# Output weights converted during the expert stage, weight sums kept for a second pass, rounds alternating at two entries, activation sums moved to VectorE

## The chip, the cores and the metric

The kernel runs on one core of one Trainium2 chip. The metric is the device time of one execution in microseconds (us), the median of several runs. The engines are TensorE (PE, matrix products), VectorE (DVE), ScalarE (ACT), GpSimd (POOL) and SyncE (SP, which here issues nearly all DMAs, in order). SBUF is the on-chip memory, PSUM the banks in which PE accumulates and from which the other engines read.

## The reference

Three stages follow one another, all in float32, on 1792 tokens of width 768:

```
scores = q @ k.T / sqrt(64) - log(448);  attn = sigmoid(scores) @ v          # 4 x 12 heads
e = argmax(x @ w_gate);  y = gate * (relu(x @ w1[e]) @ w2[e])                # 8 experts, width 1024
g = y @ w_gate2;  out = (g * sigmoid(g) * (y @ w_val)) @ w_out               # width 1536
```

w_gate2, w_val and w_out reach the kernel as 64-bit numbers and are converted to float32 on the chip with integer operations. All large products are made as three products of a value split into a high and a low part ("hi" and "lo").

## The kernel before, in words

Every engine runs its instructions in the order in which the program issues them; that order is written out by hand. Five stretches follow one another in the trace: attention (0 to about 222 us), the expert stage (to 558 us), the gated layer in two passes over the tokens (558 to 918 us), and the output product (918 us to the end).

**Expert stage.** Tokens are gathered into slots of 128. `seq` lists weight chunks, first the 6 chunks of w1 (1024 wide) of a slot, then the 8 of w2 (768 wide) of the slot before. For each chunk `split_w` makes the high part on ACT (`whi`, L936) and the low part on DVE (`wlo`, L938), and `product` (L960) multiplies. Other work is hung on places of `seq` by `when`. Among it are five half slots of 64 tokens, whose matmuls (`bps`, L1066) need no splitting: they take PE's time and nothing of DVE or ACT.

**Gated layer.** It uses Strassen's method with 7 products for 8. A round r is one column pair of w_gate2 (even r) or w_val (odd r) against one half of the tokens; there are NR = 24 rounds, the first 12 (a pass) on tokens 0 to 895, the other 12 on the rest. Each of the 7 products n of a round is 9 matmuls of 448 columns (L805, banks pa, pb, pc, pd). `steps` lists the 168 products in the order in which PE makes them. Around each product stand: `load_item` (a weight tile `w` from DRAM, on SP), `sum_w` (POOL adds weight blocks to `sr`, L695), `prep` (ACT `wgh`, DVE `wgl`, L78 and L79, five products ahead), `split_x` (the high part `x` on ACT, the low part on DVE or POOL, L779, needed at each pass's first use of a product's activations), and `evac` and `finish_tile` behind a product (PSUM banks copied out or added, then the sigmoid `m`, then `m` times value, then `h`, which SP stores in `hd`). The activations come into `rx` by PE transposes (L753) and ACT copies; their Strassen differences are made by `sum_x` (L769), on POOL for the first pass and on DVE, 1344 wide, for the second.

**w_out.** The conversion of w_out has 12 pieces of 128x768. `load_o` loads one, `convert_o` runs three steps (one ACT operation L161, four DVE operations L162 to L172, one POOL multiplication L173), and SP stores the result in `wod`. The pieces are hung on products of the gated layer, from round 5 on, 9 products apart.

**PSUM banks.** pc and pd are held by two rounds at a time; the next pair's product into a bank waits until the last reader of the pair before has read it. For products 3 and 4 that reader is the DVE addition L859 into an SBUF tile `c`.

Of the kernel before, what the change touches and what calls it, by code (L numbers as in the profile page):

```python
# [22 lines left out]
def sigmoid_attention_moe_swiglu_kernel(  # L23
# [48 lines left out]
    wgd = dram.tile([2 * K2, P, DM], F32, name="wgd")  # L72

# [82 lines left out]
    def convert(r, u, w, eng=nc.gpsimd):  # L156
# [12 lines left out]
        def s2():  # L169
            nc.vector.scalar_tensor_tensor(u, lo, 29, u, op0=ALU.logical_shift_right,  # L170
                                           op1=ALU.bitwise_or)
            eng.tensor_scalar(w, w, TINY, None, op0=ALU.is_ge)  # L172
            nc.gpsimd.tensor_tensor(w, w, u.bitcast(F32), op=ALU.mult)  # L173

        return [s0, s1, s2]

    with ExitStack() as actx:
# [28 lines left out]
        fwt = const.tile([P, G, W], F32, name="fwt")  # L206
# [473 lines left out]
    witems = [(r, x) for r in range(NR) for x in range(2)]  # L680
    full = [max(place[r, n] for n in ORD) for r in range(NR)]

    def load_item(r, x):
        t = early.tile([P, DM], F32, tag="w", name="w", bufs=4)
        f = 2 * (r // 2 % NP) + x
        nc.sync.dma_start(t, wgd[(r % 2) * K2 + f])
        wraws[r, x] = t

    def a_block(r, i, k):
        return wraws[r, i - 1][:, (k - 1) * HK:k * HK]  # L690

    def sum_w(r, n):
        def made(m, x, y, op):
            t = early.tile([P, HK], F32, tag="sr", name="sr", bufs=4)
            nc.gpsimd.tensor_tensor(t, x, y, op=op)  # L695
            sums[r, m] = t

        if n == 6:
            made(1, a_block(r, 2, 1), a_block(r, 2, 2), ALU.add)
            made(2, sums[r, 1], a_block(r, 1, 1), ALU.subtract)  # L700
        elif n == 7:
            made(3, a_block(r, 1, 1), a_block(r, 2, 1), ALU.subtract)
        elif n == 3:
# [14 lines left out]
    def load_to(m):  # L718
        while state["load"] < min(m, len(witems)):
            load_item(*witems[state["load"]])  # L720
            state["load"] += 1

    def prep_to(m):
        m = min(m, len(steps))
        while state["sum"] < min(m + 4, len(steps)):
            sum_w(*steps[state["sum"]])
            state["sum"] += 1
        while state["prep"] < m:
            prep(*steps[state["prep"]])
            state["prep"] += 1  # L730

# [16 lines left out]
    def x_piece(p, t, j):  # L748
# [8 lines left out]
        nc.scalar.copy(rx[p][:, j // K3, t, j % K3], pt[:, :TH])  # L757

    def x_block(p, k, t):
        return rx[p][:, k - 1, t - 1]  # L760

    def sum_x(p, m, eng, t=None):
        x, y = {1: lambda: (x_block(p, 1, 2), x_block(p, 1, 1)),
                2: lambda: (x_block(p, 2, 2), tr[p, 1]),
                3: lambda: (x_block(p, 2, 2), x_block(p, 1, 2)),
                4: lambda: (x_block(p, 2, 1), tr[p, 2])}[m]()
        if t is None:
            t = {3: y, 4: x}[m]
        eng.tensor_tensor(t, x, y, op=ALU.subtract)  # L769
        tr[p, m] = t  # L770
# [66 lines left out]
    def evac(r, n):  # L837
# [177 lines left out]
    pre = [lambda: load_to(4)] + [lambda m=m: prep_to(m) for m in range(1, AHEAD + 2)]  # L1015
# [89 lines left out]

    def extra():
# [38 lines left out]
    def early_sums():  # L1145
        for m in (1, 2):
            sum_x(0, m, nc.gpsimd, yt([P, K3, TH], f"t{m}"))
        sum_x(0, 3, nc.gpsimd)

    when(1, L - 1, 7, early_sums)  # L1150
    when(1, L, 4, lambda: sum_x(0, 4, nc.gpsimd))
    with tc.manual_schedule():
# [94 lines left out]
        ot = {}  # L1247

        def load_o(f):
            ot[f] = yt([P, 2 * DM], "ro64", I32)  # L1250
            load_r64(ot[f], ("o", f))

        def convert_o(f, g):
            if g == 0:
                t = yt([P, 2, DM], "uw", I32)
                w = t[:, 1].bitcast(F32)
                ot[f] = (convert(ot[f], t[:, 0], w, nc.vector), w)
            parts, w = ot[f]
            parts[g]()
            if g == 2:  # L1260
                nc.sync.dma_start(wod[f], w)
                del ot[f]

# [5 lines left out]
        R1 = 2 * NP  # L1269
        def split_all(p, n, eng=nc.gpsimd):  # L1270
# [9 lines left out]
        def sum_next(m):  # L1280
            tag = {1: "hh", 2: "hh", 4: "hl"}.get(m)
            sum_x(1, m, nc.vector, None if tag is None else post.tile(
                [P, K3, TH], F32, tag=tag, name=f"t{m}", bufs=2))

        for m in range(1, 5):
            at_step(5 + m, 5, lambda m=m: sum_next(m))
# [27 lines left out]
        def advance(r, n):  # L1314
# [6 lines left out]
            load_to(4 + 2 * sum(m <= i + AHEAD for m in full))  # L1321
# [78 lines left out]
```

## Time and profile before

| | |
|---|---|
| median of 3 runs | 1107.53 us (1107.26 to 1107.55) |
| profiled execution | 1106.29 us, its span 1104.6 us |
| mean granted clock of PE over the span | 0.98 of full speed |
| PE busy | 1044.2 us, 95% of the span |
| DVE, ACT, POOL busy | 743.0, 566.5, 444.5 us |
| DMA | 199.22 MB, mean 180 GB/s |

How to read it: an engine's busy time is summed over the whole span, and the stretches differ. PE at 95% can still have short stretches in which it waits or runs at a lower clock; those are found by cutting the span into windows. In a window's row the first figure is its length, then come each engine's busy time and instruction count, then the clock granted to PE as a share of full speed, the busy share of the DMA engines, and what they moved.

### The profile page before, as it was taken

How to read it: one execution, taken by the hardware profiler on the slowest of the kernel's cores; microseconds unless marked ns; L12 is line 12 of the kernel's file. 1: busy time of each engine (PE TensorE's matmuls, PEld its weight loads, DVE VectorE, ACT ScalarE, POOL GpSimd, SP SyncE). 2: the span in 40 equal slices, each digit the busy share in tenths (PEclk: the TensorE clock that was granted, in tenths of full speed). 3: DMA queues.
4: the chain of work that ended last, by engine and by line, in shares of the span. 5: the costliest groups of instructions: out<-in, count | busy, mean ns of one | idle time of the engine just before them, and what ended most of it. 6: DMA issues, size and time to landing. Idle time of an engine off the chain costs nothing. (4 is left out here: it accounts for less than half of the span.)

```text
span 1104.6 us, 16743 instructions
## 1 busy us (share of the span) xinstructions
PE 1044.2 (95%) x5766; PEld 846.6 (77%) x5766; DVE 743.0 (67%) x1067; ACT 566.5 (51%) x860; POOL 444.5 (40%) x348
## 2 busy tenths in 40 slices
PE   8999999999999999999779998968999999999996
PEld 5555555477868777778669997867887888999996
DVE  4777777786767767766777679999899985111110
ACT  6676766376777776767554453463344453112110
POOL 3656566420131112010475446676657663111111
PEclk9999999999999999999889999988999999999998
DMA  7897986956687757596313435423535476322210
GB/s 211 260 292 237 277 250 197 353 163 197 229 306 269 256 175 236 205 365 187 125 59 128 141 105 176 134 86 120 176 134 176 134 205 196 97 86 86 89 68 29
DMA packets 144620, 199.22 MB, mean 180 GB/s; under 512 B 54208, under 2 KB 107456, under 8 KB 144528
## 3 DMA queue, kind: packets, MB, share of 16 engines
q1 hardware_dynamic: 137552, 168.93, 48.3%
q0 software_dynamic: 6048, 28.92, 7.0%
q8 instruction: 47, 0.77, 0.3%
q14 instruction: 45, 0.37, 0.1%
q10 hardware_dynamic: 928, 0.23, 0.1%
HBM read 207.27 MB, written 42.68 MB: 226 GB/s over the span
## 5 line engine op out<-in xcount | busy, mean ns | idle before, releaser
L938 DVE TENSOR_TENSOR wlo<-wraw,whi 128x768 fp32r<-128x768 f32 (+1 forms) x186 | 199.3, 1094 | 91.9 <-ACT whi L936 89.0
L936 ACT CAST whi<-wraw 128x768 fp32r<-128x768 f32 (+1 forms) x186 | 169.9, 927 | 97.8 <-PE yps L960 50.2
L1343 PE MATMUL po<-x,hh 128*128 128x384 f32 x588 | 131.5, 336 | 1.3 <-DVE h L833 0.7
L236 ACT ACTIVATE a<-sc,logs 112x896 f32<-112x896 f32 x96 | 92.0, 1019 | 60.1 <-PE sc L234 60.1
L79 DVE TENSOR_TENSOR hl<-ht,hh 128x1536 fp32r<-128x1536 f32 x14 | 24.6, 1758 | 124.8 <-ACT hh L78 124.8
L1343 PEld LDWEIGHTS po<-x,hh 128*128 128x128 f32 x588 | 104.8, 188 | 2.0 <-DVE h L833 1.1
L805 PE MATMUL pa<-x,wgh 128*128 128x448 f32 x288 | 87.8, 386 | 18.9 <-DVE m L829 10.9
L805 PE MATMUL pd<-x,wgh 128*128 128x448 f32 x288 | 87.7, 387 | 18.0 <-DVE c L852 17.5
L79 DVE TENSOR_TENSOR wgl<-sr,wgh 128x384 fp32r<-128x384 f32 x96 | 80.3, 842 | 13.1 <-ACT wgh L78 13.1
L805 PE MATMUL pc<-x,wgh 128*128 128x448 f32 x288 | 84.4, 373 | 3.8 <-POOL x L779 2.2
L78 ACT CAST hh<-ht 128x1536 fp32r<-128x1536 f32 x14 | 20.7, 1478 | 121.1 <-PE po L1343 121.1
L172 POOL TENSOR_SCALAR w<-w 128x768 f32<-128x768 f32 x24 | 55.3, 2303 | 60.4 <-ACT w L161 60.2
L1343 PE MATMUL po<-x,hl 128*128 128x384 f32 x294 | 77.8, 336 | 0.0
L805 PEld LDWEIGHTS pa<-x,wgh 128*128 128x128 f32 x288 | 55.6, 197 | 28.6 <-DVE m L829 14.2
L245 PE MATMUL pu<-a,vraw 112*64 112x448 f32 x384 | 77.5, 545 | 0.0
L1365 POOL DMA_INDIRECT out_dram<-ob,perm_c x13 | 20.9, 1606 | 139.9 <-ACT ob L1364 139.9
L805 PEld LDWEIGHTS pd<-x,wgh 128*128 128x128 f32 x288 | 55.6, 198 | 26.9 <-DVE c L852 17.7
L79 DVE TENSOR_TENSOR wgl<-w,wgh 128x384 fp32r<-128x384 f32 x72 | 65.2, 906 | 14.0 <-ACT wgh L78 14.0
L695 POOL TENSOR_TENSOR sr<-w 128x384 f32<-128x384 f32 x48 | 60.4, 1258 | 26.2 <-DMA w<-wgd 17.7
L78 ACT CAST wgh<-sr 128x384 fp32r<-128x384 f32 x96 | 48.8, 512 | 38.9 <-PE pd L805 25.0
L805 PEld LDWEIGHTS pc<-x,wgh 128*128 128x128 f32 x288 | 54.4, 190 | 9.8 <-POOL x L779 2.6
L853 POOL TENSOR_TENSOR c<-u,c 128x448 f32<-128x448 f32 x24 | 38.9, 1621 | 55.0 <-DVE c L852 55.0
(283 smaller groups left out, 2453.6 us busy)
## 6 DMA issues: line engine op xcount, KB each, us to landing
wraw<-in_moe_w_dram SPq DMA_DIRECT2D x108, 384.0 KB
wraw<-in_moe_w_dram SPq DMA_DIRECT2D x78, 512.0 KB
w<-wgd SPq DMA_DIRECT2D x48, 384.0 KB
ring<-in_moe_w_dram SPq DMA_DIRECT2D x30, 512.0 KB
ring<-in_moe_w_dram SPq DMA_DIRECT2D x40, 384.0 KB
hd<-h SPq DMA_DIRECT2D x48, 224.0 KB
ht<-hd SPq DMA_DIRECT2D x14, 768.0 KB
r<-in_moe_w_gate_dram SPq DMA_DIRECT2D x12, 768.0 KB
```

The lines of the kernel that those rows point to most:

```text
L78: nc.scalar.copy(hi, src)
L79: nc.vector.tensor_sub(lo, src, hi.bitcast(F32))
L172: eng.tensor_scalar(w, w, TINY, None, op0=ALU.is_ge)
L236: nc.scalar.activation(am[i][:, c], sc[:CP, :, :S], AF.Sigmoid, bias=logs[:CP], scale=SCALE)
L245: nc.tensor.matmul(pu[h * D:(h + 1) * D, :S], vt[:, h, c], a[:, c, h], start=(c == 0), stop=(c == C - 1))
L695: nc.gpsimd.tensor_tensor(t, x, y, op=op)
L805: nc.tensor.matmul(ps, st[:, a], mv[:, j], start=(j == 0 and m == 0 and n not in (2, 3, 4)), stop=(j == K3 - 1 and m == 2), skip_group_che ...
L853: nc.gpsimd.tensor_tensor(t, sb[r, "u"], t, op=ALU.add)
L936: nc.scalar.copy(hi[:, :w], r)
L938: nc.vector.tensor_sub(lo[:, :w0], r[:, :w0], hi[:, :w0].bitcast(F32))
L1343: nc.tensor.matmul(po[:, m, :HW], st[:, f], wo[f, m][mv], start=(f == 0 and x == 0), stop=(f == K2 - 1 and x == 2))
L1365: nc.gpsimd.indirect_dma_start(out=out[:, :], out_offset=bass.IndirectOffsetOnAxis(ap=perm_c[:, t:t + 1], axis=0), in_=ob[:, :], in_offset ...
```

## The change

Six things are edited.

- **w_out's conversion.** Nine of the 12 pieces (FO = 9) go to the expert stage, at 18 places of `seq` that have a half slot's matmuls (`spots`): two DVE operations at each, and the ACT operation at every second one. They work in a tile `room`, which uses the space that `rx` takes later. SP gets their loads (768 KB each) and stores (384 KB each) there. The other three stay in the gated layer, in the second pass, 14 products apart. The last step is one DVE operation instead of one of DVE and one of POOL.
- **Weight sums.** In the first pass SP stores each of the 48 sums in `wsd` (192 KB each), and in the second pass it loads them from there. POOL makes no sums in the second pass, and the second `w` tile of a round is loaded by half. `sr` has 6 buffers instead of 4, and `load_more` loads a tile as soon as the one four earlier has no reads left.
- **Order of products.** At the entry of both passes, and in the last pair of the first pass, the two rounds of a pair alternate (r, r+1, r, r+1, ...). The splits of the first pass's x are hung on rounds 0, and all are on DVE.
- **Activation sums.** They are made in pieces of 448 on DVE (`t_piece`) in both passes; the first is taken by DVE from the transposes in PSUM.
- **PSUM.** For n = 3 and 4 the addition goes back into the bank, and the sigmoid and both multiplications read the bank.
- `fwt`, a table of the attention, lies in another pool.

```diff
+    wsd = dram.tile([K2, 4, P, DM // 2], F32, name="wsd")
...
+        def s3():
+            nc.vector.scalar_tensor_tensor(w, w, TINY, u.bitcast(F32), op0=ALU.is_ge,
+                                           op1=ALU.mult)
...
+    ORD2 = (1, 6, 5, 7, 2, 4, 3)
+    R1 = 2 * NP
+    BOTH = (0, R1 - 2, R1)
     steps = [(r, n) for n in ORD[:1] + ORD[4:5] for r in range(2)]
-    steps += [(r, n) for r in range(2) for n in ORD if n not in (ORD[0], ORD[4])]
-    steps += [(r, n) for r in range(2, NR) for n in ORD]
+    steps += [(r, n) for n in ORD2 if n not in (ORD[0], ORD[4]) for r in range(2)]
+    for r in range(2, NR, 2):
+        if r in BOTH:
+            steps += [(r + x, n) for n in ORD2 for x in range(2)]
+        else:
+            steps += [(r + x, n) for x in range(2) for n in ORD]
...
-        def made(m, x, y, op):
-            t = early.tile([P, HK], F32, tag="sr", name="sr", bufs=4)
-            nc.gpsimd.tensor_tensor(t, x, y, op=op)
+        def made(m, f):
+            t = early.tile([P, HK], F32, tag="sr", name="sr", bufs=6)
+            at_ = wsd[r % R1, m - 1]
+            if r < R1:
+                x, y, op = f()
+                nc.gpsimd.tensor_tensor(t, x, y, op=op)
+            else:
+                nc.sync.dma_start(t, at_)
...
+        if m is not None and r < R1:
+            nc.sync.dma_start(wsd[r, m - 1], s)
...
+        if t == 1 and k == 0:
+            nc.vector.tensor_sub(x[:, 0, 1, jj], pt[:, :TH], x[:, 0, 0, jj])
+            tr[p, 1] = x[:, 0, 1]
+        else:
+            nc.scalar.copy(x[:, k, t, jj], pt[:, :TH])
...
+    def t_piece(p, m, jj):
...
+        nc.vector.tensor_sub(tr[p, m][:, jj], x[:, jj], y[:, jj])
...
-            t = et("c", 3)
-            V.tensor_add(t, bank(r, {3: "c", 4: "d"}[n]), sb[r, "u"])
+            t = bank(r, {3: "c", 4: "d"}[n])
+            V.tensor_add(t, t, sb[r, "u"])
...
+    FO = 9
...
+    spots = [BG0 + k * BGN + d for k in range(NH0) for d in (5, 11, 18, 25, 31)]
...
+    for f in range(FO):
+        for g in range(4):
+            when(*seq[spots[2 * f + g // 2]], lambda f=f, g=g: convert_o(f, g, get_o))
...
-    when(1, L - 1, 7, early_sums)
-    when(1, L, 4, lambda: sum_x(0, 4, nc.gpsimd))
...
-        for n, at_ in ((5, (1, 2)), (7, (0, 6)), (3, (0, 5)), (4, (0, 7))):
-            at_step(*at_, lambda n=n: split_all(0, n))
+        for n in ORD2[2:]:
+            if n != 2:
+                at_step(0, {5: 6, 7: 5, 4: 7, 3: 4}[n], lambda n=n: split_all(0, n))
...
-        for f in range(K2):
-            d = 9 * f
-            at_step(5, 4, lambda f=f: load_o(f), d)
-            for g in range(3):
-                at_step(6, 4, lambda f=f, g=g: convert_o(f, g), d + g)
+        for f in range(FO, K2):
+            d = 14 * (f - FO)
+            at_step(R1 + 1, 4, lambda f=f: load_o(f, yt), d)
+            for g in range(4):
+                at_step(R1 + 2, 4, lambda f=f, g=g: convert_o(f, g), d + 2 * g)
```

How the instructions of an engine are queued, before and after, at the three places that matter. Line numbers are those of each file: L938 before is L980 after, L79 is L80, L779 is L821, L846 is L888, L852 is L894, L859 is L901.

DVE in the expert stage at two of the 18 places, before (`wlo` is the low part of an expert's weight chunk, `hl` and `xl` the low parts of activations):

```order
L938 TENSOR_TENSOR wlo<-wraw,whi 128x768
L79 TENSOR_TENSOR hl<-pt,hh 128x512 x2
L938 TENSOR_TENSOR wlo<-wraw,whi 128x768 x5
L79 TENSOR_TENSOR xl<-pt,xh 128x512
L79 TENSOR_TENSOR xl<-pt,xh 128x256
L938 TENSOR_TENSOR wlo<-wraw,whi 128x768 x2
L938 TENSOR_TENSOR wlo<-wraw,whi 128x1024 x6
```

The same place after (`room` holds the piece of w_out):

```order
L80 TENSOR_TENSOR hl<-pt,hh 128x512 x2
L980 TENSOR_TENSOR wlo<-wraw,whi 128x768
L163 TENSOR_SCALAR room<-room 128x768
L167 SCALAR_TENSOR_TENSOR room<-room 128x768
L980 TENSOR_TENSOR wlo<-wraw,whi 128x768 x4
L80 TENSOR_TENSOR xl<-pt,xh 128x512
L80 TENSOR_TENSOR xl<-pt,xh 128x256
L980 TENSOR_TENSOR wlo<-wraw,whi 128x768 x2
L171 SCALAR_TENSOR_TENSOR room<-room 128x768
L178 SCALAR_TENSOR_TENSOR room<-room 128x768
L980 TENSOR_TENSOR wlo<-wraw,whi 128x1024 x6
```

Two conversion operations stand between low parts of weights, twice in a slot; the weights behind them wait for them.

DVE at the entry of the second pass, before (`x` are the low parts of the activations, `uw` the conversion of w_out, `u`, `c`, `m`, `h` the work behind the products):

```order
L859 TENSOR_TENSOR c<-pd,u 128x448
L779 TENSOR_TENSOR x_5868<-rx,x_5867 128x448 x2
L170 SCALAR_TENSOR_TENSOR uw<-ro_8633,uw 128x768
L172 TENSOR_SCALAR uw<-uw 128x768
L79 TENSOR_TENSOR wgl<-sr,wgh 128x384
L829 TENSOR_TENSOR m<-c,m 128x448
L779 TENSOR_TENSOR x_7234<-t_8300,x_7233 128x448 x2
L79 TENSOR_TENSOR wgl<-w,wgh 128x384
L829 TENSOR_TENSOR m<-c,m 128x448
L846 TENSOR_TENSOR u<-pb,p 128x448
```

The same place after:

```order
L901 TENSOR_TENSOR pd<-pd,u 128x448
L875 TENSOR_TENSOR h<-pc,m 128x448
L80 TENSOR_TENSOR wgl<-sr,wgh 128x384
L875 TENSOR_TENSOR h<-pd,m 128x448
L821 TENSOR_TENSOR x_5935<-rx,x_5934 128x448 x3
L80 TENSOR_TENSOR wgl<-sr,wgh 128x384 x2
L888 TENSOR_TENSOR u<-pb,p 128x448
L821 TENSOR_TENSOR x_7306<-t_8222,x_7305 128x448 x3
L80 TENSOR_TENSOR wgl<-w,wgh 128x384
L888 TENSOR_TENSOR u<-pb,p 128x448
```

The conversion is gone from there, all three splits of a set are DVE's (POOL had the third), and two rounds' work behind the products comes between two sets.

POOL near the end of the second pass, before (`sr` the weight sums, `uw` the last step of the conversion):

```order
L695 TENSOR_TENSOR sr<-w 128x384
L695 TENSOR_TENSOR sr<-w,sr 128x384
L853 TENSOR_TENSOR c<-u,c 128x448
L695 TENSOR_TENSOR sr<-w 128x384
L695 TENSOR_TENSOR sr<-sr,w 128x384
L829 TENSOR_TENSOR m<-c,m 128x448
L695 TENSOR_TENSOR sr<-w 128x384
L173 TENSOR_TENSOR uw<-uw 128x768
```

And after:

```order
L895 TENSOR_TENSOR c<-u,c 128x448
L871 TENSOR_TENSOR m<-c,m 128x448
L895 TENSOR_TENSOR c<-u,c 128x448
L875 TENSOR_TENSOR h<-c,m 128x448
L895 TENSOR_TENSOR c<-u,c 128x448
L871 TENSOR_TENSOR m<-c,m 128x448
```

Only the work behind product 7 is left on POOL there.

## Rows read from the trace of the kernel before

**Rows 1.** Windows by stage: length, busy us per engine, PEclk, DMA share, GB/s.

```profile
core 0: us, PE busy (x) PEld busy (x) DVE busy (x) ACT busy (x) POOL busy (x), PEclk, DMA share, GB/s
245.00:455.00 210.00, 208.63 (x1099) 159.33 (x1099) 149.06 (x163) 148.99 (x198) 33.59 (x39) 1.00 0.70 240
530.00:558.20 28.20, 20.79 (x99) 18.08 (x97) 20.83 (x17) 12.98 (x22) 17.70 (x9) 0.88 0.20 67
558.20:579.80 21.60, 16.11 (x55) 13.63 (x56) 18.58 (x24) 12.69 (x28) 14.91 (x12) 0.76 0.23 73
579.80:654.80 75.00, 75.00 (x393) 68.56 (x392) 51.87 (x78) 34.01 (x71) 37.93 (x33) 1.00 0.44 138
654.80:728.60 73.80, 67.29 (x324) 59.78 (x322) 71.96 (x86) 36.84 (x75) 49.38 (x35) 1.00 0.36 121
728.60:764.10 35.50, 23.62 (x86) 19.86 (x85) 34.50 (x44) 12.25 (x26) 27.00 (x19) 0.76 0.41 138
764.10:900.90 136.80, 130.29 (x619) 116.56 (x618) 127.93 (x164) 59.14 (x115) 91.38 (x64) 0.99 0.47 153
900.90:917.70 16.80, 13.67 (x64) 11.60 (x63) 13.55 (x21) 10.99 (x24) 8.49 (x8) 1.00 0.78 233
```

**Rows 2.** Windows by stage, PE's L805 matmuls alone: length, busy us (count).

```profile
579.80:654.80 75.00, 73.01 (x345) 1.00 0.44 138
```

**Rows 3.** Chain of waits, 598 to 640 us: start, us, engine, products of nine.

```profile
601.97 1.82 PE pa L805 x9
605.64 0.39 PE pt L753 x4
620.83 1.86 PE pc L805 x9
```

**Rows 4.** Waits of PE, 558 to 918 us: total us, times, longest.

```profile
PE pd L805 <- DVE c L852: 17.5, 9, 8.4
PE pa L805 <- DVE m L829: 10.9, 8, 2.4
```

**Rows 5.** Timeline of PE, 730 to 765 us: start, us, idle before.

```profile
737.35 1.11 PE L805 MATMUL pd<-x,wgh 128*128 128x448 f32 x2 [8.39 <-DVE c L852]
738.26 0.57 PE L805 MATMUL pd<-x,wgl 128*128 128x448 f32 x1
...
743.59 0.37 PE L805 MATMUL pa<-x,wgl 128*128 128x448 f32 x1
```

**Rows 6.** Waits of PE, 500 to 558 us.

```profile
PE pa L805 <- DVE x L779: 6.6, 2, 4.8
```

**Rows 7.** Timeline of DVE, 534 to 554 us.

```profile
535.02 7.34 DVE L779 TENSOR_TENSOR x<-rx,x 128x448 fp32r<-128x448 f32 x3
...
549.38 0.62 DVE L779 TENSOR_TENSOR x<-rx,x 128x448 fp32r<-128x448 f32 x1
```

**Rows 8.** Timeline of POOL, 530 to 560 us.

```profile
534.35 3.62 POOL L769 TENSOR_TENSOR t<-rx,t 128x1344 f32<-128x1344 f32 x1
```

**Rows 9.** DVE groups, 654 to 918 us, shapes apart: count, busy, mean ns, idle before.

```profile
L79 DVE TENSOR_TENSOR wgl<-sr,wgh 128x384 fp32r<-128x384 f32 x67 | 61.4, 922 | 1.1 <-ACT wgh L78 1.1
L829 DVE TENSOR_TENSOR m<-c,m 128x448 f32<-128x448 f32 x18 | 21.5, 1196 | 0.0
...
L166 DVE SCALAR_TENSOR_TENSOR uw<-ro,uw 128x768 int32<-128x768 int32 x12 | 12.8, 1067 | 0.0
...
L829 DVE TENSOR_TENSOR m<-pa,m 128x448 f32<-128x448 f32 x9 | 5.5, 607 | 0.0
```

**Rows 10.** Timeline of DVE, 614 to 625 us.

```profile
619.40 0.61 DVE L833 TENSOR_TENSOR h<-c,m 128x448 f32<-128x448 f32 x1
619.93 0.55 DVE L79 TENSOR_TENSOR wgl<-sr,wgh 128x384 fp32r<-128x384 f32 x1
```

**Rows 11.** DVE groups, 245 to 455 us, shapes apart.

```profile
L938 DVE TENSOR_TENSOR wlo<-wraw,whi 128x768 fp32r<-128x768 f32 x72 | 67.8, 959 | 36.2 <-ACT whi L936 35.4
```

**Rows 12.** Timeline of PE, 395 to 426 us.

```profile
419.46 2.79 PE L1066 MATMUL bps<-ring,xbt 128*64 128x512 f32 x12
```

More of the change, by code (lines that the diff above doesn't have):

```diff
@@ L205, in sigmoid_attention_moe_swiglu_kernel @@
         pairs = [(b, g) for b in range(B) for g in range(G)]
-        fwt = const.tile([P, G, W], F32, name="fwt")
+        fwt = rp.tile([P, G, W], F32, name="fwt")
         n = len(pairs)
@@ L714, in prep, with load_more, sum_to @@
         wst[r, n] = (hi, lo)
+        if m is not None and r < R1:
+            nc.sync.dma_start(wsd[r, m - 1], s)
     state = {"load": 0, "sum": 0, "prep": 0, "now": 0}
-    def load_to(m):
-        while state["load"] < min(m, len(witems)):
-            load_item(*witems[state["load"]])
-            state["load"] += 1
+    def load_more():
+        while state["load"] < len(items):
+            k = state["load"] - NW
+            if k >= 0 and left[items[k]]:
+                break
+            load_item(*items[state["load"]])
+            state["load"] += 1
+    def sum_to(m):
+        load_more()
+        while state["sum"] < min(m, len(steps)) and (steps[state["sum"]][0], 1) in wraws:
+            sum_w(*steps[state["sum"]])
+            state["sum"] += 1
     def prep_to(m):
         m = min(m, len(steps))
-        while state["sum"] < min(m + 4, len(steps)):
-            sum_w(*steps[state["sum"]])
-            state["sum"] += 1
         while state["prep"] < m:
+            sum_to(state["prep"] + 5)
             prep(*steps[state["prep"]])
             state["prep"] += 1
+        sum_to(m + 4)
     rows = {}
@@ L1013, in sigmoid_attention_moe_swiglu_kernel @@
             when(1, s - 3, GJ, lambda s=s: gather(s))
-    pre = [lambda: load_to(4)] + [lambda m=m: prep_to(m) for m in range(1, AHEAD + 2)]
+    pre = [load_more] + [lambda m=m: prep_to(m) for m in range(1, AHEAD + 2)]
     for i, f in enumerate(pre):
@@ L1024, in sigmoid_attention_moe_swiglu_kernel @@
         when(1, L - 1, j, lambda j=j: x_piece(0, 1, j))
+    for j in range(K3):
+        for m, c in ((2, L * KF - 2 + j), (3, L * KF + 1 + j), (4, L * KF + 4 + j)):
+            when(1, c // KF, c % KF, lambda m=m, j=j: t_piece(0, m, j))
     bgw = {}
@@ L1104, in sigmoid_attention_moe_swiglu_kernel, with load_o, convert_o, get_o @@
     when(*seq[BG0 - 4], lambda: [bg_load(n) for n in range(RB)])
+    ot = {}
+    FO = 9
+    def load_o(f, get):
+        ot[f] = get([P, 2 * DM], "ro64", I32)
+        load_r64(ot[f], ("o", f))
+    def convert_o(f, g, get=yt):
+        if g == 0:
+            t = get([P, 2, DM], "uw", I32)
+            w = t[:, 1].bitcast(F32)
+            ot[f] = (convert(ot[f], t[:, 0], w, True), w)
+        parts, w = ot[f]
+        parts[g]()
+        if g == 3:
+            nc.sync.dma_start(wod[f], w)
+            del ot[f]
+    spots = [BG0 + k * BGN + d for k in range(NH0) for d in (5, 11, 18, 25, 31)]
+    room = {}
+    def get_o(shape, name, dt):
+        if not room:
+            room["t"] = early.tile([P, 4 * K3 * TH], I32, tag="rx", name="room", bufs=1)
+        k = room[name] = room.get(name, -1) + 1
+        if name == "ro64":
+            return room["t"][:, k % 2 * 2 * DM:(k % 2 + 1) * 2 * DM]
+        return room["t"][:, 4 * DM:6 * DM].rearrange("p (a d) -> p a d", a=2)
+    for f in range(FO):
+        for g in range(4):
+            when(*seq[spots[2 * f + g // 2]], lambda f=f, g=g: convert_o(f, g, get_o))
+        if f < 2:
+            when(*seq[spots[0] - 6], lambda f=f: load_o(f, get_o))
+        else:
+            when(*seq[spots[2 * f - 3] + 1], lambda f=f: load_o(f, get_o))
     def extra():
@@ L1245, in split_wo @@
                     load_wo(f + 4)
[L1247 to L1262, printed above, removed]
         todo = {}
@@ L1279, in sigmoid_attention_moe_swiglu_kernel @@
                 at_step(3 + 2 * t, ORD[j + 1], lambda t=t, j=j: x_piece(1, t, j))
[L1280 to L1286, printed above, removed]
+        for m in range(2, 5):
+            for j in range(K3):
+                at_step(4 + m, ORD[1 + 2 * j], lambda m=m, j=j: t_piece(1, m, j))
         for n in ORD:
@@ L1320, in advance @@
             prep_to(i + 1 + AHEAD)
-            load_to(4 + 2 * sum(m <= i + AHEAD for m in full))
         strassen(0, 2)
```

63 lines of the change are left out of this document (33 added, 30 removed).

## Prediction

> **What bounds the kernel now.** I read the windows by stage first, then PE's waits, then the timelines at those waits. PE sets the end, but not everywhere by its own work. In the middle of the first pass it is busy for all of 75.00 us, and there a product of nine matmuls takes 1.82 to 1.86 us [rows 1 to 3]; I take 1.843, 0.2048 a matmul. What each stretch of the gated layer would need at that rate is its matmul count (PE's count in the row; in the 75 us stretch 345 of 393 are products) times 0.2048, and the rest is lost [rows 1, 2]:
>
> - entry, 558.2 to 579.8: 21.6 - 55 x 0.2048 = 10.3 us
> - 579.8 to 654.8: 75.0 - 345 x 0.2048 = 4.3, which the 12 groups of four transposes at 0.39 fill [rows 3]: 0
> - 654.8 to 728.6: 73.8 - 66.4 = 7.4
> - change of pass, 728.6 to 764.1: 35.5 - 17.6 = 17.9
> - 764.1 to 900.9: 136.8 - 126.8 = 10.0
> - to 917.7: 16.8 - 13.1 = 3.7
>
> That is 49.3 us. A further stretch is the end of the expert stage, 530 to 558.2: PE is busy for 20.8 of 28.2 us, at a clock of 0.88 [rows 1]; 7.4 idle and 12% of 20.8 make 9.9. So 59.2 us can be had at most without fewer matmuls, and nothing in the change touches the output product.
>
> Who makes PE wait is plain: DVE. In the bad stretches DVE is busy for 71.96 of 73.8 and 34.5 of 35.5 us, in the good one for 51.87 of 75 [rows 1]. PE waits 17.5 us for the addition behind product 7 and 10.9 for m [rows 4]; both stand late in DVE's queue. [...]
>
> DVE is late for two reasons. It has too many operations there, and they are slowed by POOL: three splits took 7.34 us beside a POOL subtraction of 3.62, while one alone takes 0.62 [rows 7, 8]; wgl takes 922 ns on average in the second half against 0.55 in a quiet place [rows 9, 10]; m from SBUF takes 1196 ns and the same from PSUM 607 [rows 9].
>
> **The change part by part.**
>
> *Sums out of the second pass, conversion out of both.* Second pass: POOL loses its 48 sums and all conversion multiplies, DVE loses 9 of 12 pieces. Per piece DVE has four operations, before and after; at 1067 ns [rows 9] as upper end, 4.3 us, so 38 us of DVE go out of 654 to 918, and out of the 136.8 us stretch, where some six pieces lie and three will, 13. With the sums gone wgl and m fall towards 0.55 and 0.61 there: the stretch has 619 / 9 = 69 wgl, at most 69 x 0.37 = 25 us, and some 12 m from SBUF, 7 us; I take 20 of these 32. DVE then has 128 - 13 - 20 = 95 of 136.8 us, 69%, the good stretch's share [rows 1]. I leave 1.5 of its 10.0 us lost, 1 of the 7.4 (sums stay there, the conversion goes), 0.5 in the good stretch, where the sums' stores are new on SP, and 2 of the end's 3.7, since the split of output weights stays.
>
> *Change of pass.* The wait of 8.39 us comes from splits, conversion, three 1344-wide subtractions and evacuations in one queue. Alternating rounds give two products' time, 3.7 us, to each set of three splits (1.9 at 0.62) plus two wgl (1.1) plus evacuation (0.6 to 1.2): 3.6 to 4.2. Just enough, so I leave 2.5 of 17.9, one short wait with its slow matmuls; the bounds are 0 and 10, the loss of the entry as it is.
>
> *End of the expert stage.* PE's 6.6 us of waiting for x [rows 6] fall where POOL subtracts. DVE now makes these sums in nine pieces; at the 0.62 of a split that is 5.6 us, spread over as many places. I leave 4 of 9.9 (bounds 1 and 9.9): they come between the last low parts of expert weights.
>
> *First entry.* In the first products after the alternating start DVE has 12 splits (7.4), 8 wgl (4.4) and 6 evacuations (3.7) = 15.5 us, and PE needs 14.7 for eight products. DVE still sets this, and the clock is at 0.76 there [rows 1]. Four splits come back from POOL, where they were no faster. I leave 7 of 10.3, bounds 2 and 10.3, nearer to the row as it stands.
>
> *Conversion in the expert stage.* Added there: 36 DVE operations 768 wide, at wlo's 959 ns [rows 11] 34.5 us, and 9 on ACT, some 8. DVE has 149 of 210 us busy, so 184, 87%; ACT 75% [rows 1]. The cover is the half slots' matmuls: 2.79 us for one chunk [rows 12], without anything to split, and DVE was idle 36.2 us before these wlo's, waiting for ACT [rows 11]. Two operations are 1.9 us. Queued behind them are the next low parts, for which PE would wait. I take 2 us for all 18 places; the bounds are 0 and 42 (all of it bare). The 10.6 MB of DMAs add 50 GB/s to 240, at a share of 0.70 [rows 1]; on SP they stand ahead of expert weights, which are loaded a slot ahead.
>
> *PSUM banks held longer.* Products 3 and 4 now leave their bank only when h has been read. In the row, h of pc ends at 620.01, and the next pair's pc starts at 620.83 [rows 3, 10]: 0.8 us of room. Where h comes later the wait is PE's. No row shows it; bounds 0 and about 17 (below), I take 3 for a few short ones. In return m and h of these products read PSUM at 607 ns, not SBUF at 1196 [rows 9].
>
> [...] The trace has m from PSUM at 607 ns, and a split from SBUF alone at 620 [rows 7, 9]: no difference. [...]
>
> **Sum.** Left: expert stage 2, its end 4, entry 7, 0.5 + 1, change of pass 2.5, 1.5, end 2, banks 3: 23.5 us. Gain 59.2 - 23.5 = 35.7. The profiled execution had 1106.29, so 1070.6; the median of the runs is 1.24 above it: 1071.8.
>
> **Rivals.**
>
> A, the forecast: 1060 to 1084, the sum with entry, change of pass and expert stage each a few us off. 0.66.
>
> B, late hand-offs. For: SP issues in order, and a load of a sum can stand behind a store of h that waits for DVE or POOL; and the banks wait for h. Each of the 11 other pair changes then costs 0.8 to 1.5 us and, being short, now and then some slow matmuls: 9 to 17, to 28 with the clock. 1084 to 1100. Against: only 0.8 us has to be missed for a few, and six buffers of sums stand ready. 0.16.
>
> C, all waits go: DVE keeps to the good stretch's 69% everywhere, and PE runs through. 1107.5 - 59.2 = 1048 to 1060. Against: the entry has 15.5 us of DVE for 14.7 of PE. 0.11.
>
> D, slower. The conversion in the expert stage lies bare: the ACT operation waits until the room's last store has left, wlo's are held behind it on both engines, and PE, which has 208.6 of 210 us there, waits at each of 18 places. Outside that stage the gain is 37.7 us, so 2.1 us a place breaks even; 3 us, one piece's ACT operation and two of DVE in full, gives 1071.8 - 2 + 54 = 1124. For: DVE at 87% in a chain ACT, DVE, PE. Against: the 36.2 us of DVE's idle time and the half slots' matmuls at the same places. 0.05.
>
> E, the change does nothing: what leaves DVE's queue is not what PE waited for, and the waits turn up elsewhere in it: 1107. Rows 4 speak against it. 0.02.
>
> **How the numbers follow.** Predicted 1071.8, the likeliest case. Its own range is 1060 to 1084; taking in most of B and C, with D and E and the outer tails left out, 1052 to 1092. Faster by over 0.2%, about what a measurement of this kernel can tell: A + B + C = 0.93; within 0.2%: 0.02; slower: 0.05.
>
> **What would show it.** In the changed profile: DVE busy under 75% from 764 us on and wgl there near 0.6 us; no PE wait over 2 us at the change of pass and a clock near 1.0; the entry still 4 us or more over its matmul count; in the expert stage PE waits for wlo or whi under 3 us in all, with DVE at 85%; at changes of pair, PE's waits for h under 0.5 us each. Wrong would make it: PE waits for room operations or whi at the 18 places (D), regular waits for h or for sums at pair changes (B), or a first entry as fast as its matmuls (C).

## The result and the profile after

The changed kernel takes 1065.22 us, median of 4 runs (1063.58 to 1067.04), against 1107.54 before: ratio 0.9614, 95% interval 0.9594 to 0.9635. That is 42 us faster; 1071.8 was predicted, with 1052 to 1092 as its range. The profiled execution took 1067.04 us (span 1065.3), 39.3 less than the one before.

Where the time went is read best from the start of the same product of the gated layer in both traces. The 168 products are counted from 0 in the order in which PE makes them; 0 and 1 stand among the last work of the expert stage. One trace per kernel is read here, and at the first entry (products 4 to 18) traces differ by some us even where the queues are the same, as the run copy_out shows below.

| product starts | before, us | after, us | after is ahead by | gained since the row above |
|---|---|---|---|---|
| 0 (in the expert stage) | 533.30 | 534.93 | -1.6 | -1.6 |
| 4 | 560.17 | 555.48 | 4.7 | 6.3 |
| 14 | 588.88 | 578.33 | 10.6 | 5.9 |
| 54 | 667.36 | 662.16 | 5.2 | -5.4 |
| 70 | 702.57 | 691.61 | 11.0 | 5.8 |
| 98 | 774.63 | 744.56 | 30.1 | 19.1 |
| 160 | 898.88 | 858.61 | 40.3 | 10.2 |
| start of the output product | 918.45 | 878.60 | 39.9 | -0.4 |

The windows by stage of the changed kernel, cut at these products (columns as in [rows 1]; the first is the expert stage, the second its end, then the first entry, two stretches of the first pass, the change of pass, the second pass, the end):

```profile
249.40:456.60 207.20, 205.41 (x1079) 156.16 (x1080) 177.56 (x197) 153.87 (x204) 42.30 (x40) 1.00 0.82 292
527.60:555.48 27.88, 24.76 (x135) 21.68 (x132) 20.22 (x31) 17.31 (x30) 4.81 (x5) 1.00 0.41 137
555.48:578.33 22.85, 19.91 (x92) 16.43 (x91) 21.29 (x31) 11.85 (x27) 12.73 (x11) 1.00 0.38 123
578.33:649.28 70.95, 67.91 (x346) 61.21 (x345) 44.41 (x79) 30.37 (x64) 33.68 (x30) 0.98 0.60 188
649.28:715.80 66.52, 66.45 (x325) 60.71 (x324) 57.00 (x85) 34.65 (x73) 35.55 (x28) 1.00 0.45 146
715.80:733.50 17.70, 17.10 (x82) 14.96 (x82) 15.42 (x30) 8.53 (x19) 0.00 (x0) 1.00 0.28 91
733.50:860.40 126.90, 126.90 (x622) 116.34 (x621) 89.96 (x153) 56.77 (x112) 28.20 (x21) 1.00 0.58 190
860.40:878.60 18.20, 15.34 (x65) 12.87 (x63) 14.62 (x24) 12.14 (x26) 8.10 (x8) 0.91 0.72 223
```

In the second pass PE is never idle until the last eight products: 126.90 of 126.90 us, the clock at 1.00. The clock of 0.76 at entry and change of pass is gone; products 14 to 20, just behind the entry, still have 0.90. The longest of PE's waits left in the gated layer (total us, times, longest; compare [rows 4]):

```profile
PE pa L847 <- DVE m L871: 2.1, 1, 2.1
PE pd L847 <- DVE h L875: 1.9, 1, 1.9
PE pd L847 <- DVE c L894: 1.7, 2, 0.9
PE pd L847 <- DVE m L871: 1.1, 2, 0.7
```

17.5 us for c and 10.9 for m became 1.7 and 3.2, and a wait of 1.9 for h is new. That one stands at the first pair change, where the first product of rounds 2 and 3 needs the bank that rounds 0 and 1 still hold. PE's timeline shows it with slow matmuls behind it:

```profile
586.84 0.76 PE L847 MATMUL pd<-x,wgh 128*128 128x448 f32 x2 [1.88 <-DVE h L875]
587.41 0.57 PE L847 MATMUL pd<-x,wgl 128*128 128x448 f32 x1
```

Two of DVE's groups in the second pass, the low part of the weights and m from PSUM, are to be compared with [rows 9]. Of the two behind them, from the expert stage, the first is the low part of expert weights, to be compared with [rows 11], and the second one operation of the conversion:

```profile
L80 DVE TENSOR_TENSOR wgl<-sr,wgh 128x384 fp32r<-128x384 f32 x42 | 25.4, 606 | 18.0 <-ACT wgh L79 17.9
L871 DVE TENSOR_TENSOR m<-pc,m 128x448 f32<-128x448 f32 x6 | 3.7, 617 | 0.0
```

```profile
L980 DVE TENSOR_TENSOR wlo<-wraw,whi 128x768 fp32r<-128x768 f32 x72 | 69.6, 983 | 20.0 <-ACT whi L978 18.4 <-DMA ring<-in_moe_w_dram 0.7
L167 DVE SCALAR_TENSOR_TENSOR room<-room 128x768 int32<-128x768 int32 x9 | 8.6, 959 | 0.3
```

In the second pass wgl went from 927 ns to 606 (the 922 of [rows 9] takes in a part of the first pass). Three of the conversion's four kinds of operation took the 950 to 960 ns that wlo's row had promised, and the fourth (L163) took 553, so all 36 cost 30.8 us of DVE. Its idle time before 768-wide wlo's fell from 36.2 to 20.0 us.

### The profile page after: what moved, and what is told of

It reads as the page before. It is cut to its first block, busy times and chain, and to the rows that moved or that the text cites. A ratio compares the mean times of both kernels' runs of the same rounds, so it can differ in the third digit from the quotient of the medians.

```text
span 1065.3 us, 16836 instructions
## 1 busy us (share of the span) xinstructions
PE 1034.1 (97%) x5766; PEld 841.3 (79%) x5766; DVE 696.9 (65%) x1098; ACT 562.9 (53%) x854; POOL 327.7 (31%) x273
## 5 line engine op out<-in xcount | busy, mean ns | idle before, releaser
L980 DVE TENSOR_TENSOR wlo<-wraw,whi 128x768 fp32r<-128x768 f32 (+1 forms) x186 | 198.4, 1089 | 57.8 <-ACT whi L978 53.3
L80 DVE TENSOR_TENSOR hl<-ht,hh 128x1536 fp32r<-128x1536 f32 x14 | 24.6, 1759 | 127.6 <-ACT hh L79 127.6
L847 PE MATMUL pd<-x,wgh 128*128 128x448 f32 x288 | 84.3, 374 | 5.3 <-DVE h L875 1.9
L847 PE MATMUL pa<-x,wgh 128*128 128x448 f32 x288 | 83.0, 370 | 3.4 <-DVE m L871 2.1
L80 DVE TENSOR_TENSOR wgl<-sr,wgh 128x384 fp32r<-128x384 f32 x96 | 62.9, 660 | 35.4 <-ACT wgh L79 35.3
L895 POOL TENSOR_TENSOR c<-u,c 128x448 f32<-128x448 f32 x24 | 35.6, 1488 | 160.3 <-DVE c L894 154.6
L79 ACT CAST hh<-ht 128x1536 fp32r<-128x1536 f32 x14 | 20.7, 1477 | 121.3 <-PE po L1397 121.3
L79 ACT CAST wgh<-sr 128x384 fp32r<-128x384 f32 x96 | 49.0, 514 | 36.5 <-PE pd L847 18.9
L1002 PE MATMUL yps<-whi,hh 128*128 128x384 f32 x216 | 58.7, 352 | 0.0
L1002 PE MATMUL yps<-wlo,hh 128*128 128x384 f32 x216 | 56.3, 341 | 2.0 <-DVE wlo L980 1.9
```

The costliest lines, as they stand in the source:

```text
L79: nc.scalar.copy(hi, src)
L80: nc.vector.tensor_sub(lo, src, hi.bitcast(F32))
L847: nc.tensor.matmul(ps, st[:, a], mv[:, j], start=(j == 0 and m == 0 and n not in (2, 3, 4)), stop=(j == K3 - 1 and m == 2), skip_group_che ...
L895: nc.gpsimd.tensor_tensor(t, sb[r, "u"], t, op=ALU.add)
L980: nc.vector.tensor_sub(lo[:, :w0], r[:, :w0], hi[:, :w0].bitcast(F32))
L1002: nc.tensor.matmul(ps[:, m, :w], st[:, a], mv[:, m * w:(m + 1) * w], start=(j == 0 and i == 0), stop=(j == m_ - 1 and i == 2))
```

## The experiments

The theory is that PE waits in the gated layer because DVE's queue is late: operations taken out of it (conversion), made shorter (no POOL beside them) or given more time (alternating rounds) each return part of the time. Its rivals are that single parts do nothing, or that the expert stage pays. Ratios are to the kernel before on the same chip; the change has 0.9614. 0.001 is 1.1 us.

**The conversion back in the gated layer** (conv_back).

```diff
-    FO = 9
+    FO = 0
-            d = 14 * (f - FO)
-            at_step(R1 + 1, 4, lambda f=f: load_o(f, yt), d)
+            d = 9 * f
+            at_step(5, 4, lambda f=f: load_o(f, yt), d)
             for g in range(4):
-                at_step(R1 + 2, 4, lambda f=f, g=g: convert_o(f, g), d + 2 * g)
+                at_step(6, 4, lambda f=f, g=g: convert_o(f, g), d + min(g, 2))
```

> The changed kernel with all 12 pieces of w_out's conversion back in the gated layer, from round 5 on, 9 products apart, as before. Theory (DVE's queue is what PE waits for in the gated layer): 36 DVE operations of about 1 us come back between 650 and 860 us, and DVE goes from 71% to about 85% there; the waits come back at the change of pass, where nothing is left over, not in the middle of a pass. 1072 to 1082 against 1065, with PE waits for c, m or x of 5 to 12 us between products 54 and 98. Rival (the conversion was hidden anyway, and its move buys nothing once the sums are out): 1063 to 1067. Second rival (the move costs in the expert stage): below 1063.

1090.26 us, ratio 0.983 (0.9808 to 0.9852): 24 us of the gain go, more than any case had. PE waits for c, m and h again, as the theory has it, but not only where it said: 9.2 us are lost in products 70 to 98, around the change of pass, and 11.0 in 98 to 160, in the middle of the pass, where it expected none.

**The conversion alone moved, in the kernel before** (b_conv): `convert`, `room` and `spots` as in the change, nothing else.

> The kernel before with this one part of the change alone: nine pieces of the conversion in the expert stage at the same 18 places, three in the second pass, fused last step. Theory: the expert stage loses 0 to 2 us; in the gated layer DVE loses 9 of 12 pieces, but POOL's sums still slow it, so the stretches 655 to 729 and 764 to 901 get back most of their 17 us and the change of pass some of its 18: 1085 to 1095. Rival (the parts only help together, since DVE stays the bound while the sums run): 1098 to 1107. Second rival (the conversion lies bare in the expert stage): above 1107.

1081.92 us, ratio 0.9759 (0.9734 to 0.9784): 26.7 us, more than the theory had (1085 to 1095). One part alone brings nearly two thirds of the whole, and undoing it costs nearly as much. The two kernels differ in a way that corrects the reading of shares. The same stretch in conv_back, then in b_conv (columns as above):

```profile
765.00:880.00 115.00, 108.94 (x520) 98.47 (x521) 86.39 (x145) 50.70 (x101) 22.40 (x16) 0.99 0.64 207
```

```profile
765.00:880.00 115.00, 112.97 (x547) 103.02 (x546) 98.42 (x135) 52.49 (x102) 65.13 (x50) 0.99 0.42 140
```

In b_conv DVE is busier (98.4 us of 115, 86%, against 86.4, 75%; 0.73 us an operation against 0.60, with POOL busy for 65.1 us against 22.4) and PE still runs better: products 98 to 160 take 114.5 us there, 125.1 in conv_back and 114.1 in the changed kernel. So it isn't DVE's share that makes PE wait, but what stands in its queue ahead of m, h and the additions. This is DVE's timeline of conv_back, just ahead of a pair change:

```profile
758.93 0.95 DVE L171 SCALAR_TENSOR_TENSOR uw<-ro,uw 128x768 int32<-128x768 int32 x1
759.92 0.96 DVE L178 SCALAR_TENSOR_TENSOR uw<-uw 128x768 f32<-128x768 f32 x1
760.80 0.55 DVE L80 TENSOR_TENSOR wgl<-sr,wgh 128x384 fp32r<-128x384 f32 x1
761.26 0.63 DVE L901 TENSOR_TENSOR pd<-pd,u 128x448 f32<-128x448 f32 x1
...
764.44 0.61 DVE L875 TENSOR_TENSOR h<-pd,m 128x448 f32<-128x448 f32 x1
```

and PE, to which this queue hands the banks:

```profile
765.20 0.65 PE L847 MATMUL pc<-x,wgh 128*128 128x448 f32 x2 [2.32 <-DVE h L875]
769.03 0.65 PE L847 MATMUL pd<-x,wgh 128*128 128x448 f32 x2 [1.74 <-DVE h L875]
```

Two conversion operations of 0.95 and 0.96 us stand ahead of the addition, and with it the sigmoid on ACT and h move back past the pair change. That these two cause the wait is read from the order of the queue. conv_back has the last two operations of a piece at one product, while the change and b_conv have two products between them; no run separates the number of pieces from this spacing.

**The weight sums on POOL in both passes** (sums_back). The second weight tile of a round is loaded whole again.

```diff
...
-            if r < R1:
+            if True:
                 x, y, op = f()
...
-        if m is not None and r < R1:
-            nc.sync.dma_start(wsd[r, m - 1], s)
```

> The changed kernel with POOL making the weight sums in the second pass too, nothing stored or loaded for them. Theory (POOL's sums slow DVE where the two meet): wgl in the second pass goes from 0.57-0.61 us back to above 0.8, but with only three conversions left there DVE stays under 90%, so PE loses little in the middle of the pass and some at its entry, which is where DVE is short: 1067 to 1075. Rival (the sums in the second pass are the larger half of the gain): 1078 to 1088. Second rival (the sums cost nothing, the loads on SP do): 1060 to 1065.

1074.98 us, ratio 0.9698 (0.9676 to 0.9719): 9.3 us, at the upper end of the theory's range. wgl in the second pass rose to 796 ns. The place is only in part the theory's: 4.0 us are lost in products 70 to 98, and 7.0 in 98 to 160, the middle of the pass, where it expected little. The stored sums are worth less than the conversion.

**No alternation at the second entry** (seq_entry2): `BOTH = (0,)`.

> The changed kernel with rounds alternating at the first entry only; the last pair of the first pass and the first pair of the second are made round after round. Theory: each set of three splits then has one product's time (1.84 us for 1.9 of splits plus wgl plus evacuation) over the first seven products, DVE falls behind by about 1.2 us a product, and a stall of 4 to 8 us with slow matmuls behind it comes back at the change of pass: 1071 to 1079. Rival (with conversion and subtractions out of the way DVE keeps up anyway): 1064 to 1067.

1072.92 us, ratio 0.9684 (0.9662 to 0.9706): 7.8 us, as the theory had it. PE waits for h up to 3.3 us at the change of pass.

**First pass's differences on POOL** (pool_sums_x).

```diff
-            when(1, c // KF, c % KF, lambda m=m, j=j: t_piece(0, m, j))
+    when(1, L - 1, 7, lambda: [t_pool(2), t_pool(3)])
+    when(1, L, 4, lambda: t_pool(4))
```

> The changed kernel with the activation differences 2, 3 and 4 of the first pass on POOL again, 1344 wide, at their old places; the first still from PSUM on DVE. Theory (POOL's wide subtractions lock out DVE's splits, three of which took 7.34 us beside one): the end of the expert stage loses its gain, PE waits for x again by 4 to 7 us, 1069 to 1073. Rival (the gain there comes from the splits being moved to other places and to DVE alone): 1064 to 1067.

1070.6 us, ratio 0.9655 (0.9635 to 0.9676): 4.5 us, and PE's one wait for x of 4.8 us is back. DVE and POOL of this kernel, then DVE of the changed one at the same set of splits:

```profile
535.14 4.50 DVE L821 TENSOR_TENSOR x<-rx,x 128x448 fp32r<-128x448 f32 x3
```

```profile
534.47 3.62 POOL L1072 TENSOR_TENSOR t<-t,rx 128x1344 f32<-128x1344 f32 x1
```

```profile
534.54 1.69 DVE L821 TENSOR_TENSOR x<-rx,x 128x448 fp32r<-128x448 f32 x3
```

Three splits took 4.50 us beside POOL's operation and 1.69 without, and the 4.50 end 1.55 us after that operation.

**The additions copied out to SBUF** (copy_out).

```diff
-            t = bank(r, {3: "c", 4: "d"}[n])
-            V.tensor_add(t, t, sb[r, "u"])
+            t = et("c", 3)
+            V.tensor_add(t, bank(r, {3: "c", 4: "d"}[n]), sb[r, "u"])
```

> The changed kernel with the additions behind products 3 and 4 written to an SBUF tile again, so that a bank is free after the addition, not after h. Theory (the bank hand-off is short only at the first pair change, 0.73 + 1.88 us of PE waiting for h and 1.3 us of slow matmuls; everywhere else there is room): products 14 to 18 take about 7.4 us instead of 11.7, the rest is the same: 1060 to 1064. Rival (m and h from SBUF meet POOL's operations and take up to 1.2 us instead of 0.61, so DVE gets late): 1066 to 1075.

1061.32 us, ratio 0.957 (0.9549 to 0.9591): 3.9 us better than the change by the medians and 4.9 by the ratios, the two intervals just apart. In its trace products 14 to 18 take 7.37 us instead of 11.69, as expected, but products 4 to 14 take 27.5 instead of 22.9, with a wait of 3.39 us for c. But the entry has two courses, and these two traces do not share one. These rows are the second set of splits from rx and the POOL sum next to it, in the changed kernel, then in conv_back, whose queues there are the same:

```profile
566.20 1.68 DVE L821 TENSOR_TENSOR x<-rx,x 128x448 fp32r<-128x448 f32 x3
567.98 1.22 POOL L717 TENSOR_TENSOR sr<-w 128x384 f32<-128x384 f32 x1 [6.19 <-DVE x L821]
```

```profile
564.55 1.36 POOL L717 TENSOR_TENSOR sr<-w 128x384 f32<-128x384 f32 x1 [4.55 <-DVE x L821]
564.98 4.11 DVE L821 TENSOR_TENSOR x<-rx,x 128x448 fp32r<-128x448 f32 x3
```

Where POOL's sums start ahead of this set, the set takes about 4 us (conv_back, pool_sums_x, copy_out, best2); where they start behind it, 1.7 (the change, shifted, doubled, seq_entry2, conv_copy). Only traces with the same course should be compared. With the long set, products 4 to 18 take 36.9 and 35.6 us in conv_back and pool_sums_x, which add in PSUM, against 34.9 and 33.7 in copy_out and best2. With the short set, they take 33.7 to 34.8 in the four that add in PSUM, against 31.3 in conv_copy. By these few traces copying out saves some 1 to 3 us at the entry; in both copy_out and best2 it saves 1.1 at the change of pass. Of the parts that were undone, summing in PSUM is the one that does not pay.

**Both of these** (conv_copy).

> Two edits: all 12 pieces of the conversion back in the gated layer (as in the run of that edit alone, 1090), and the additions behind products 3 and 4 copied out to SBUF (alone 1061). Theory (the conversion's operations stand ahead of m and h in DVE's queue, and with the sums added in PSUM the banks wait for that h, so the late queue costs more than it did before): without the hold the conversion costs well under the 25 us that it costs alone: 1074 to 1083. Rival (the delays reach PE by other ways, m of product 2 and the addition behind product 7, as much): the two effects add up, 1090 - 4 = 1084 to 1090.

1083.78 us, ratio 0.9762 (0.9739 to 0.9785), at the border of the two ranges. Beside copy_out the conversion costs 0.0192, 21 us, and beside the change 24. So most of its cost does not come through the held banks; with copy-out PE waits 9.4 us for m and 7.0 for c.

**The 18 places moved three chunks, away from the half slots' matmuls** (shifted).

```diff
-for d in (5, 11, 18, 25, 31)]
+for d in (8, 14, 21, 28, 34)]
```

> The changed kernel with the 18 places moved three chunks later, to where there are no half slots' matmuls; the operations are the same. Theory (the cover is the idle time spread over the whole stretch, since the low parts are made two chunks ahead): the expert stage grows by 0 to 4 us: 1064 to 1069. Rival (the half slots' matmuls at the same places are the cover): 18 places at 1 to 1.9 us, 1083 to 1100, with PE waits for wlo at each.

1081.32 us, ratio 0.9747 (0.973 to 0.9764). The same work costs 15 us more in the expert stage (product 0 starts at 549.77 instead of 534.93), 0.8 us a place. That falsifies the theory's 0 to 4 and falls short of the rival's 18 and more, with a wait at every place. So the half slots' matmuls are a cover, and DVE's idle time is another: it hid about half of the 30.8 us of operations even here. Of the 14.8 us, 8.2 are eight waits for wlo and 4.0 slow matmuls (PE is busy for 313.8 us from 222 us to product 0, instead of 309.8). The two longest waits:

```profile
368.41 0.74 PE L1002 MATMUL hps<-wlo,xh 128*128 128x512 f32 x2 [3.05 <-DVE wlo L980]
...
395.72 0.62 PE L1002 MATMUL yps<-wlo,hh 128*128 128x384 f32 x2 [1.89 <-DVE wlo L980]
```

Ahead of the longer one DVE had this operation beside two weight sums of POOL, at 1.83 us instead of 0.96, so a part of that wait is POOL's and not the missing cover's:

```profile
364.60 1.83 DVE L178 SCALAR_TENSOR_TENSOR room<-room 128x768 f32<-128x768 f32 x1
```

**Twice as many DVE operations at the 18 places** (doubled): two more of 128x768 into unused columns at each.

> The changed kernel with two more VectorE operations of the conversion's kind (128x768, into unused columns) at each of the 18 places in the expert stage, 36 in all, about 34 us of DVE; they add work and change no result. Theory (the cover is DVE's idle time before the low parts, 27.6 us left in the changed kernel): DVE would need 212 of 207 us, so it becomes the bound there, and PE waits for wlo: the expert stage grows by 6 to 20 us: 1071 to 1085. Rival (each place has a cover of its own of 2.2 to 2.8 us of half slots' matmuls, and what exceeds it, 3.5 - 2.5 = 1.0 us, is paid 18 times whatever DVE's idle time): 1083 to 1090, with waits at every place alike. Second rival (nothing shows, DVE has more room than the rows say): 1064 to 1067.

1076.85 us, ratio 0.9709 (0.9691 to 0.9727): 10.5 us, 0.6 us a place for 1.9 us of added work. That is in the range of the theory by idle time, which shifted had contradicted, and below the rival's 1.0 a place; neither account holds alone. Where the place is right, doubling the work costs less than the plain work three chunks later.

**POOL's work behind product 7 of the first pair on DVE** (entry_dve).

```diff
-            nc.gpsimd.tensor_tensor(t, sb[r, "u"], t, op=ALU.add)
-            finish_tile(k + 2, r, 2, 2, t, nc.gpsimd)
+            g = V if r < 2 else nc.gpsimd
+            g.tensor_tensor(t, sb[r, "u"], t, op=ALU.add)
+            finish_tile(k + 2, r, 2, 2, t, g)
```

> The changed kernel with POOL's work behind product 7 of rounds 0 and 1 (two additions, one m, one h) given to DVE; everything else is the same. Theory (at the first entry DVE's set of three splits takes 4.21 us instead of 1.9 because POOL works beside it at 571 to 578 us, and that makes h late at the first pair change): DVE does 4 x 0.61 us more, its splits are fast again, the 5 us lost between products 14 and 18 shrink to under 2: 1060 to 1063. Rival (the weight sums on POOL do the same harm, and the four operations come on top): 1065 to 1069.

1069.07 us, ratio 0.9638 (0.9615 to 0.966): no gain, rather 2.7 us worse, but the intervals overlap. That is the upper end of the rival's range. The set of splits that had 4.21 us in the changed kernel fell to 1.69, the one before it took 3.29 beside weight sums, and products 4 to 18 took 38.0 us instead of 34.5. POOL's sums start ahead of the set here, as in conv_back and pool_sums_x, which take 36.9 and 35.6, so less of the 3.5 us may be the edit's.

**Without the weight sums of rounds 2 and 3** (no_sums): a block of weights is loaded in place of each sum, so these two rounds multiply other weights.

> The changed kernel without the eight weight sums of rounds 2 and 3, which POOL makes while DVE splits x at the first entry; a block of weights is loaded in place of each, so these two rounds multiply other weights. Theory (what is left of the entry's loss, products 4 to 18 in 34.5 us where PE needs 25.8, is POOL's sums slowing DVE): sets of three splits take 1.7 to 2 us instead of 4.2, products 4 to 18 take 28 to 31, and the whole 1059 to 1063. Rival (DVE has 15.5 us for 14.7 of PE there, so it stays late with POOL silent too): products 4 to 18 in 33 to 35, the whole 1064 to 1067.

1068.49 us, ratio 0.9623 (0.9598 to 0.9649): nothing won. Products 4 to 18 take 32.4 us, between the theory's 28 to 31 and the rival's 33 to 35: 2.2 less than in the change, and 1.4 to 2.4 less than in the four traces with sums and the short set. The set of splits beside POOL's work behind product 7 still takes 3.61 us, the one before it, with POOL idle, 1.70. What is won goes in a new wait of 3.96 us for m, at product 21, and its chain leads to a DMA: DVE's m stands behind a wgl, this waits for ACT, and ACT for one of the blocks loaded in place of the sums. ACT's timeline, and the window of that load:

```profile
592.69 0.51 ACT L79 CAST wgh<-sr 128x384 fp32r<-128x384 f32 x1 [4.85 <-DMA sr<-wgd]
```

```profile
585.00:590.00 5.00, 5.00 (x27) 4.59 (x26) 1.23 (x3) 1.06 (x2) 1.40 (x1) 1.00 0.97 282
```

The load was issued by 585.9, and the DMA engines are 97% busy in that window. The total of this run is therefore no measure of the entry; the product times are, if roughly: of 8.7 us lost between products 4 and 18 of the change, the sums account for some 2.

**Copy-out, and the first two tiles of the output product split some 14 products earlier** (best2).

```diff
-            at_step(NR - 3, 7, lambda t=t: load_h(t), t)
-            at_step(NR - 2, 7, lambda t=t: split_h(t), t)
+            at_step(NR - 5, 7, lambda t=t: load_h(t), 3 * t)
+            at_step(NR - 4, 7, lambda t=t: split_h(t), 5 * t)
```

> Copy-out of the additions behind products 3 and 4 (alone 1061), and the first two tiles of the output product's left factor loaded and split some 14 products earlier, away from the last pair, where PE waits 2.1 us for m of product 2 behind two hl operations of 1.76 us each and falls to the lower clock. Theory: the last eight products lose 2 to 4 us less: 1057 to 1060. Rival (what delays m there is the split of the output weights on POOL beside DVE, not the hl operations): 1060 to 1063.

1060.72 us, ratio 0.9556 (0.9535 to 0.9577), the best of all, 0.6% below the change, its interval apart from the change's. The total lies in the rival's range, 0.7 us above the theory's, and its step over copy_out, 0.0014, is too small for the intervals. The traces speak for the theory: from product 160 to the output product it is 17.2 us instead of copy_out's 19.2, and the 2.1 us wait for m is gone, as expected.

## Why the prediction was right

The sum held nearly term by term: none is off by more than 2.6 us, and the errors cancel only in part. The table has the gain of each stretch, forecast and measured from product starts. The cuts are the products nearest to those of [rows 1], but for the end of the first entry, which is cut at product 14, where both kernels have made the same products:

| | forecast | measured |
|---|---|---|
| expert stage | -2 | -1.6 |
| its end | 5.9 | 6.3 |
| first entry | 3.3 | 5.9 |
| bank hand-offs, and sums' stores to 655 us | -3.5 | -5.4 |
| 655 to 729 us | 6.4 | 7.8 |
| change of pass | 15.4 | 16.9 |
| second pass | 8.5 | 10.4 |
| end | 1.7 | -0.4 |
| sum | 35.7 | 39.9 |

- **Who bounds.** That it is DVE's queue is confirmed from both sides by conv_back and b_conv, the one 24 us worse than the change, the other 27 better than the kernel before. But the argument by DVE's share, "69%, the good stretch's share", was right by luck: 71% came (89.96 of 126.9), but conv_back's 75% lost 11 us in products 98 to 160 and b_conv's 86% under one.
- **Which half.** The prediction put relief by POOL's silence (20 of 33 us of DVE's time in the second pass) above the conversion's 13. Undone one at a time, the conversion is worth 24 us, the sums 9, alternating at the second entry 8, the differences on DVE 4.5, and summing in PSUM costs 5: the order of the two halves was wrong. These add up to 41 of the 42, but alternating at the first entry was not undone, so whether the parts overlap is not shown.
- **Expert stage.** "2 us for all 18 places" was met: -1.6, of which 0.7 was there when the stage's first half slot began. DVE is busy for 86% of it (87 forecast). The half slots' matmuls and DVE's idle time both cover the operations, as the prediction had it; shifted and doubled show that neither does it alone. The working had one slip: the 2.79 us of [rows 12] are a place's whole group, three chunks, not one.
- **First entry and banks.** These two terms belong together, and their sum was met: 3.3 - 3.5 = -0.2 forecast, 0.5 measured. Apart, neither was right. At product 9, where the bad stretch of the row ended, the change was 13.6 us ahead, and by product 21 it had lost 7.6 of that again. In this trace the clock did not fall in products 4 to 14 (1.00); in conv_back, with the same queues there, it fell to 0.82, and these products took 5.8 us more, of which 2.4 were left at product 18. So it is in part luck of the one execution that the entry beat "nearer to the row as it stands".
- **Where the banks cost.** Not a few short waits but one place, the first pair change, cost 4.3 us. The set of splits before it took 4.21 us, so h was late. At the ten other pair changes PE's waits have no h.
- **Operands in PSUM.** m from a bank took 617 ns in the changed kernel, and a split with SBUF operands alone 620 [rows 7]: the changed kernel shows no difference either.
- **End.** This is the one stretch that was forecast to gain and did not. m of product 2 stands behind two hl in DVE's queue, and PE waits 2.1 us for it; best2 took that away:

```profile
855.23 1.76 DVE L80 TENSOR_TENSOR hl<-ht,hh 128x1536 fp32r<-128x1536 f32 x1 [2.63 <-ACT hh L79]
857.90 1.75 DVE L80 TENSOR_TENSOR hl<-ht,hh 128x1536 fp32r<-128x1536 f32 x1
862.00 0.61 DVE L871 TENSOR_TENSOR m<-pa,m 128x448 f32<-128x448 f32 x1
```

- **Rival B's range.** 9 to 17 us for the banks in place of 3 give 1078 to 1086 by the prediction's own sum, and 1097 with the clock; its 1084 to 1100 does not follow from that.
- **Slow matmuls.** The 2.5 us left at the change of pass, for one short wait and slow matmuls behind it, and rival B's 11 us for the clock (28 - 17) are amounts that no run shows. The changed kernel had PE busy for 17.10 of 17.70 us at the change of pass, at a granted clock of 1.00. Matmuls at 0.57 us instead of 0.37 came in its gated layer behind two waits, the 1.88 us at the first pair change and the 2.06 at the end, for some 3 us each, at a clock of 0.50 (589 to 590 us, 863.8 to 867 us).

It is not settled what products 4 to 18 take when POOL has neither its work behind product 7 nor sums there, since no run took both away, nor what decides whether POOL's sums start ahead of the second set.

## What to carry to other kernels

Judge an engine that serves the busy one by what stands in its queue ahead of the instruction waited for, not by its share: here one at 75% cost 11 us, one at 86% under one. Work that only needs to be done at some time belongs where the busy engine has matmuls that the serving engine need not prepare; three chunks beside that place, it cost 15 us. An operation that leaves its result in the accumulator bank can cost more than it saves when a later reader then holds the bank: here some 4 to 5 us. And compare two traces of the same queues before a difference of a few us at one place is put down to an edit: here products 4 to 18 took from 33.7 to 36.9 us without one.

## What the runs showed of the hardware

Three VectorE splits of 128x448 took 1.68 to 1.70 us where GpSimd was idle (changed kernel, entry_dve, no_sums). Beside GpSimd operations of 128x384 and 128x448 they took 2.52 and 4.21 us in the changed kernel, 3.29 in entry_dve, 3.32 and 3.61 in no_sums and 4.11 in conv_back; beside subtractions of 128x1344 they took 4.50 in pool_sums_x and 7.34 in the kernel before.

The wait of 1.88 us at the first pair change was followed in the changed kernel by matmuls at 0.57 us instead of 0.37 for some 3 us, with a granted clock of 0.90 over products 14 to 20. In shifted, sums_back, seq_entry2 and pool_sums_x the same wait, of 1.87 or 1.88 us, was followed by matmuls at 0.37 at a clock of 1.00. Likewise, a wait of 3.4 us for c in products 4 to 14 went with a clock of 0.82 over them in conv_back and of 1.00 in pool_sums_x. The length of the wait alone did not decide it. PE's timeline of shifted, to be set beside the rows of the changed kernel above:

```profile
601.83 0.65 PE L847 MATMUL pd<-x,wgh 128*128 128x448 f32 x2 [1.88 <-DVE h L875]
602.32 0.37 PE L847 MATMUL pd<-x,wgl 128*128 128x448 f32 x1
```
